# Issuing the K and V loads of a decode attention from GpSimd's software queue

## The chip, the cores and the metric

The kernel runs on one core of one Trainium2 chip. The metric is the device time of one execution in microseconds (us); before the change it is 1980.17 us, the median of three runs (1979.96 to 1980.22).

## The reference

Two blocks, A and B, of one-token attention over a long cache, each with 2 batches, 32 heads, 8192 cached positions and a head size of 192, in bf16:

```
q      = x @ wq                                  # x: 2 x 1 x 640, wq: 640 x 6144
scores = einsum("bhqd,bhkd->bhqk", q, k_cache) * 192 ** -0.5
p      = softmax(scores)
o      = einsum("bhqk,bhkd->bhqd", p, v_cache)
out    = o.transpose(0, 2, 1, 3).reshape(2, 1, 6144) @ wo     # wo: 6144 x 640
```

The two outputs are joined along the last axis. Nearly all the bytes are the four caches: K and V of one head of one batch are 8192 x 192 bf16 each, 3.146 MB, and there are 128 such pairs.

## The kernel before

One pair is a *unit*; units are counted u = 0 to 127 (NU = 128), two batches of a head after each other. K and V of a unit lie in SBUF as 128 partitions of 64 positions each, 24,576 bytes a partition. There are two K buffers (`kb`, NK = 2) and three V buffers (`vb`, NV = 3).

The work on a unit goes through all engines:

- **VectorE (DVE)** multiplies K by the broadcast query, in two halves (`dve_mul`, L230; signals "m0" and "m1"). It needs K(u), and frees K's buffer when "m1" is done. Later it gathers the sums (L233, "r0", "r1") and takes the maximum of each partition (L236, "d3").
- **TensorE (PE)** sums the products over the head size with an identity matrix (`pe_sum`, L295, "s0" and "s1"), and later multiplies the probabilities with V (`pe_pv`, L306, "pv"), which frees V's buffer.
- **GpSimd (POOL)** takes the maximum over all partitions (`pool_ar`, L220, called ar here) and later sums the exponentials over them (`pool_ls`, L224, called ls here).
- **ScalarE (ACT)** scales the maximum (L243), takes the exponential (L246, "exp") and evicts results.

Each engine works through its own list in order, and a wait holds everything behind it on that engine. DVE, ACT, PE and POOL have tables with a slot for each unit; `put(table, slot, order, ...)` files an operation, and the lists are written out by slot and, within a slot, by order. POOL's slot u holds ar(u) (order 0, waits for "d3" of u) and ls(u) (order 1, waits for "exp" of u). On PE the slot u holds the sums of u (order 0) and then the V product of u - 1 (order 2). The last two units differ: the sums of units 126 and 127 stand in slot 125 at order 1.8, and so ahead of the V product of unit 124, called pv(124) here.

SyncE (SP) issues all loads from one list, made at L425 to L454. K(u) waits for "m0" and "m1" of u - 2, V(u) for "pv" of u - 3. The order is K(0), wq(0), K(1), wo(0), V(0), K(2), V(1), K(3), V(2) and so on: the V of a unit stands behind the K of the next unit. K(127) is moved up behind K(126) and split into two halves; V(126) is split in two and V(127) in four pieces. Weights are set between: wq for 8 heads (1.97 MB, 3072 bytes a row, one buffer; waits for the last query projection from the one before, "pq") and wo for 4 heads (0.98 MB, 3840 bytes a row, two buffers; waits for "f5"). The query projections (`pe_q`, L287) run six units ahead of their use. The last two wo loads go into a K buffer at the end (L453).

K's loads count on one semaphore for each buffer (`ksem`), V's likewise (`vsem`).

The order of SP's list is made by these lines:

```python
for u in range(NU):
    order.append(("k", u))
    if u >= 1:
        order.append(("v", u - 1))
order.append(("v", NU - 1))
order.remove(("k", NU - 1))
order.insert(order.index(("k", NU - 2)) + 1, ("k", NU - 1))
```

Of the kernel before, what the change touches and what calls it, by code (L numbers as in the profile page):

```python
# [51 lines left out]
def build_kernel(nc, blocks, out):  # L52
# [5 lines left out]
    TH = T // 2  # L58
# [5 lines left out]
    NU = G * B  # L64
# [3 lines left out]
    NK = 2  # L68
    NV = 3
# [12 lines left out]
    def unit(u):  # L82
        g = u // B
        return g // Hn, g % Hn, u % B, g
# [7 lines left out]
    with ExitStack() as es:  # L92
        sb = lambda name, shape, dt: es.enter_context(nc.sbuf_tensor(name, shape, dt))
        ps = lambda name, shape, dt: es.enter_context(nc.psum_tensor(name, shape, dt))
        sem = lambda name: es.enter_context(nc.semaphore(name))

        kb = [sb(f"kb{i}", [128, T, Dh], BF16) for i in range(NK)]
# [28 lines left out]
        reg = {}  # L126
        S_sp = _Stream("sp", sem("s_sp"), reg)
# [4 lines left out]
        ksem = [sem(f"ksem{i}") for i in range(NK)]  # L132
        k2sem = {NU - 1: sem("k2sem1")}
# [10 lines left out]
        def key(name, *idx):  # L144
            for i in idx:
                if i < 0:
                    return None
            return (name,) + tuple(idx)

        vcount = [0] * NV  # L150
        for u in range(NU):
            reg[("k", u)] = (ksem[u % NK], 16 * (u // NK + 1))
            if u in VSPLIT:
                for i in range(len(VSPLIT[u]) - 1):
                    reg[("vp", u, i)] = (vpsem[u, i], 16)
            else:
                vcount[u % NV] += 1
                reg[("v", u)] = (vsem[u % NV], 16 * vcount[u % NV])
# [11 lines left out]
        def dma(out_ap, in_ap, s):  # L170
            return lambda eng: eng.dma_start(out_ap, in_ap).then_inc(s, 16)  # L171
# [4 lines left out]
        def sp_wq(w):  # L176
            blk = (w * HQ) // Hn
            h0 = (w * HQ) % Hn
            src = blocks[blk]["wq"].rearrange("(j c) n -> j c n", c=DC)[:, :, h0 * Dh:(h0 + HQ) * Dh]
            return dma(wqs[:], src, wqsem)  # L180
# [10 lines left out]
        def sp_wo(w):  # L191
            blk = (w * HO) // Hn
            h0 = (w * HO) % Hn
            src = blocks[blk]["wo"][h0 * Dh:(h0 + HO) * Dh, :].rearrange("(pr p i) n -> p pr (i n)", p=128, i=3)
            i = w - (NWO - NLATE)
            return dma(wo_tile(w).rearrange("p pr i n -> p pr (i n)"), src, wosem[w % 2] if i < 0 else wlsem[i])

        def sp_k(u, part=None):
            blk, h, b, g = unit(u)
            src = blocks[blk]["k"][b, h].rearrange("(p t) d -> p t d", p=128)  # L200
            if part is None:
                return dma(kb[u % NK][:], src, ksem[u % NK])
            if part == 0:
                return dma(kb[u % NK][:, 0:TH, :], src[:, 0:TH, :], ksem[u % NK])
            return dma(kb[u % NK][:, TH:T, :], src[:, TH:T, :], k2sem[u])

        def sp_v(u, t0=0, t1=T, sm=None):
            blk, h, b, g = unit(u)
            src = blocks[blk]["v"][b, h].rearrange("(p t) d -> p t d", p=128)
            return dma(vb[u % NV][:, t0:t1, :], src[:, t0:t1, :], vsem[u % NV] if sm is None else sm)  # L210

        def vcuts(u):
            c = VSPLIT[u]
            return list(zip(c[:-1], c[1:]))
# [23 lines left out]
        def dve_f2(g):  # L238
            s0 = 64 * (g % 2)
            return lambda eng: eng.reciprocal(rcT[(g // 2) % 2][s0:s0 + 64, :], lall[g % 2][s0:s0 + 64, :])  # L240
# [8 lines left out]
        def act_f1(g, b0, b1):  # L249
            hs = g % 2  # L250

            def fn(eng):
                eng.activation(o_sb[0:1, b0:b1, hs, :], ops[hs][0:1, b0:b1, 0:Dh], ACTF.Identity)  # L253
                return eng.activation(o_sb[32:33, b0:b1, hs, :], ops[hs][32:33, b0:b1, Dh:2 * Dh], ACTF.Identity)  # L254
            return fn
# [96 lines left out]
        pool_tab = [[] for _ in range(NSLOT)]  # L352

        def put(tab, slot, order, fn, waits, sig):
            tab[slot].append((order, len(tab[slot]), fn, waits, sig))

        for u in range(NU):
# [17 lines left out]
            else:  # L375
                cuts = vcuts(u)
                for i, (t0, t1) in enumerate(cuts):
                    put(pe_tab, u + 1, 2, pe_pv(u, t0 // 2, t1 // 2), (w0 if i == 0 else []) + [("vp", u, i)],
                        ("pv", u) if i == len(cuts) - 1 else None)

        for g in range(G):
            u1 = 2 * g + 1
            pp = g // 2
            w1 = [key("f3", pp - 1), ("init",)]
            if g == G - 1:
                put(act_tab, u1, 2, act_f1(g, 0, 1), [("pv", u1 - 1)] + w1, ("f1a", g))
                put(act_tab, u1 + 1, 2, act_f1(g, 1, 2), [("pv", u1), ("f1a", g)], ("f1", g))
            else:
                put(act_tab, u1 + 1, 2, act_f1(g, 0, 2), [("pv", u1)] + w1, ("f1", g))
            put(dve_tab, u1 + 1, 8, dve_f2(g), [("ls", u1), key("f4", pp - 2)], ("f2", g))  # L390
# [41 lines left out]
        order.insert(order.index(("k", NU - 2)) + 1, ("k", NU - 1))  # L432
        for kind, u in order:
            if kind == "k":
                S_sp.add(sp_k(u, 0 if u in k2sem else None), waits=[key("m0", u - NK), key("m1", u - NK)])
                if u in k2sem:
                    S_sp.add(sp_k(u, 1))
                if u == 0:
                    S_sp.add(sp_wq(0))
                w = u // UO  # L440
                if u % UO == 1 and w < NWO - NLATE:
                    S_sp.add(sp_wo(w), waits=[key("f5", ((w - 2) * HO + HO - 1) // 2 if w >= 2 else -1)])
                w = u // UQ
                if u % UQ == UQ - LEAD and w + 1 < NWQ:
                    S_sp.add(sp_wq(w + 1), waits=[key("pq", w * HQ + HQ - 1)])
            else:
                w = [key("pv", u - NV)]
                if u in VSPLIT:
                    for i, (t0, t1) in enumerate(vcuts(u)):
                        S_sp.add(sp_v(u, t0, t1, vpsem[u, i]), waits=w)  # L450
                else:
                    S_sp.add(sp_v(u), waits=w)
# [23 lines left out]
        for tab, S in ((dve_tab, S_dve), (act_tab, S_act), (pe_tab, S_pe), (pool_tab, S_pool)):  # L476
            evicted = None
            for slot in range(NSLOT):
                for _, _, fn, waits, sig in sorted(tab[slot], key=lambda e: (e[0], e[1])):
                    if sig is not None and sig[0] in ("pq", "f3", "f3a"):  # L480
                        waits = list(waits) + [evicted]
# [27 lines left out]
def bass_concat_heads__gqa_block_cached__mha_block_cached__decode_kernel(  # L509
    nc: bass.Bass,  # L510
    A_x: bass.AP,
    A_k_cache: bass.AP,
    A_v_cache: bass.AP,
    A_wq: bass.AP,
    A_wo: bass.AP,
    B_x: bass.AP,
    B_k_cache: bass.AP,
    B_v_cache: bass.AP,
    B_wq: bass.AP,
    B_wo: bass.AP,  # L520
    out: bass.AP,
):
    blocks = [
        dict(x=A_x, k=A_k_cache, v=A_v_cache, wq=A_wq, wo=A_wo),
        dict(x=B_x, k=B_k_cache, v=B_v_cache, wq=B_wq, wo=B_wo),
    ]
    build_kernel(nc, blocks, out)
# [28 lines left out]
```

## Time and profile before

| | |
|---|---|
| median of three runs | 1980.17 us |
| span of the profiled execution, first to last instruction | 1978.0 us |
| PE busy | 1651.6 us (84%) |
| DVE busy | 1056.0 us (53%) |
| ACT busy | 191.3 us (10%) |
| POOL busy | 121.6 us (6%) |
| read from HBM | 836.77 MB, 423 GB/s over the span |

The profiled execution's own time is not given apart from its span; the median of the runs is 2.2 us longer than the span.

The profile shows one execution. "Busy" counts the time that an engine works on instructions; issuing a DMA and waiting are not in it. The slices cut the span into 40 equal parts. The line of DMA gives the busy share of the 16 DMA engines in tenths, and the line below it what they moved. The DMA issues are listed with the median time from the issue to the landing, that is, until the semaphore tells that all has arrived; this holds the time in the queue too. In a timeline, a line has the start, the time, the engine, the line of the code, the operation, output and input with their shapes, and in brackets the idle time before it and what ended it. The chain of waits goes back from the last instruction: at each step to what released it.

### The profile page before, as it was taken

To read this page: it belongs to the slowest core of one execution; us is meant where nothing else is said; L and a number is where in the kernel's file an instruction comes from. 1 tells how busy PE (TensorE), PEld (TensorE's weight loads), DVE (VectorE), ACT (ScalarE), POOL (GpSimd) and SP (SyncE) were. 2 spreads that over 40 slices of the span, in tenths; PEclk is the share of its full clock that TensorE was granted. 3 is DMA by queue.
4 is the path that set the end of the run, shared out by engine and by line. 5 is a ranking of instruction groups with operands and counts; after the bars stand their busy time and mean duration, and the time that the engine had idled before them with its cause. 6 is when DMAs were issued, how large, how long until landed. Compare 5 with 4: busy or idle time off the path is not lost.

```text
span 1978.0 us, 18521 instructions
## 1 busy us (share of the span) xinstructions
PE 1651.6 (84%) x8076; PEld 816.4 (41%) x8076; DVE 1056.0 (53%) x706; ACT 191.3 (10%) x647; POOL 121.6 (6%) x269
## 2 busy tenths in 40 slices
PE   5988888879888888888888878888788977988878
PEld 2444444334444344443444434444344433444434
DVE  4554555545555455655555556555555555556552
ACT  0100101001010010010110101001001000010000
POOL 2200000000000000000000000000000000000001
PEclk9999999999999899998999999998999899998988
DMA  9999999999999999999999999999999999999995
GB/s 402 430 429 430 429 430 431 430 429 430 430 429 429 431 429 430 431 428 430 431 429 430 427 431 431 428 431 427 432 431 427 430 430 430 430 431 429 430 405 236
DMA packets 47856, 837.96 MB, mean 424 GB/s; under 512 B 5144, under 2 KB 5152, under 8 KB 14752
## 3 DMA queue, kind: packets, MB, share of 16 engines
q1 hardware_dynamic: 47188, 836.78, 99.0%
q8 instruction: 63, 1.03, 0.2%
q14 instruction: 17, 0.14, 0.0%
q10 hardware_dynamic: 588, 0.01, 0.0%
HBM read 836.77 MB, written 0.01 MB: 423 GB/s over the span
## 4 chain that ended last, share of the span: by engine, by line
DMA 74%; DVE 11%; issue 10%; PE 4%; POOL 0%; ACT 0%; SPq 0%; DVEq 0%
DMA kb<-in_B_k_cache_dram 38%; DMA kb<-in_A_k_cache_dram 35%; DVE prod L230 11%; PE scps L295 2%; PE ops L306 2%; DMA wqs<-in_A_wq_dram 1%; PE qps L287 0%; PE outps L341 0%; POOL mg L220 0%; PE qps L325 0%; DVE sc L233 0%; ACT qbc L266 0%; ACT pb L246 0%; ACT out_sb L270 0%; SPq L171 0%
## 5 line engine op out<-in xcount | busy, mean ns | idle before, releaser
L230 DVE TENSOR_TENSOR prod<-kb,qbc 128x6144 bf16<-128x6144 bf16 x256 | 848.2, 3355 | 530.4 <-DMA kb<-in_B_k_cache_dram 265.7
L295 PE MATMUL scps<-prod,ident 128*128 128x512 bf16 x3072 | 784.5, 414 | 289.7 <-DVE prod L230 289.4
L306 PE MATMUL ops<-vb,pb 128*33 128x384 bf16 x4096 | 716.4, 335 | 11.4 <-DMA vb<-in_A_v_cache_dram 6.8
L295 PEld LDWEIGHTS scps<-prod,ident 128*128 128x128 bf16 x3072 | 306.0, 105 | 753.7 <-DVE prod L230 370.9
L306 PEld LDWEIGHTS ops<-vb,pb 128*33 128x33 bf16 x4096 | 400.7, 100 | 315.4 <-issue 63.3
L233 DVE TENSOR_REDUCE sc<-scps 128x32 f32<-128x512 f32 x256 | 176.7, 690 | 345.0 <-PE scps L295 344.2
L220 POOL PARTITION_ALL_REDUCE mg<-mp x128 | 63.7, 498 | 1710.2 <-DVE mp L236 1282.2
L243 ACT ACTIVATE nb<-mg 128x1 f32<-128x1 f32 x128 | 26.0, 203 | 1369.1 <-POOL mg L220 1369.1
L287 PE MATMUL qps<-wqs,xbc 128*128 128x384 bf16 x320 | 65.5, 337 | 22.7 <-DMA wqs<-in_A_wq_dram 17.3
L314 PEld LDWEIGHTS qps<-ones,o_sb 33*128 33x128 f32 x372 | 67.1, 257 | 13.1 <-issue 13.1
L314 PE MATMUL qps<-ones,o_sb 33*128 33x1 f32 x372 | 69.7, 311 | 0.0
L224 POOL PARTITION_ALL_REDUCE lall<-rs x128 | 53.2, 416 | 116.9 <-ACT pb L246 116.9
L253 ACT ACTIVATE o_sb<-ops 1x384 f32<-1x384 f32 (+1 forms) x65 | 30.8, 475 | 248.6 <-PE ops L306 248.6
L246 ACT ACTIVATE pb<-sc,nb 128x64 bf16<-128x64 f32 x128 | 52.3, 408 | 14.0 <-PE ops L306 9.8
L287 PEld LDWEIGHTS qps<-wqs,xbc 128*128 128x128 bf16 x320 | 26.7, 99 | 56.5 <-issue 20.5
L266 ACT ACTIVATE qbc<-qps 128x384 bf16<-128x384 f32 x64 | 31.4, 490 | 141.7 <-PE qps L287 141.0
L254 ACT ACTIVATE o_sb<-ops 1x384 f32<-1x384 f32 (+1 forms) x65 | 31.0, 476 | 0.8
L236 DVE TENSOR_REDUCE mp<-sc 128x1 f32<-128x64 f32 x128 | 28.2, 220 | 4.4
L341 PE MATMUL outps<-wos,oTz 128*4 128x320 bf16 x168 | 27.4, 299 | 0.0
L246 ACT ACTIVATION_READ_ACCUMULATOR pb<-sc,nb 128x1 f32 x128 | 23.8, 186 | 0.0
L341 PEld LDWEIGHTS outps<-wos,oTz 128*4 128x4 bf16 x168 | 11.9, 84 | 17.6 <-issue 11.9
L240 DVE RECIPROCAL rcT<-lall 64x2 f32<-64x2 f32 x64 | 9.9, 154 | 12.7 <-POOL lall L224 11.7
(21 smaller groups left out, 33.2 us busy)
## 6 DMA issues: line engine op xcount, KB each, us to landing
kb<-in_A_k_cache_dram SPq DMA_DIRECT2D x64, 3072.0 KB, 22.5
vb<-in_A_v_cache_dram SPq DMA_DIRECT2D x64, 3072.0 KB, 29.5
kb<-in_B_k_cache_dram SPq DMA_DIRECT2D x63, 3072.0 KB, 22.5
vb<-in_B_v_cache_dram SPq DMA_DIRECT2D x62, 3072.0 KB, 29.8
wqs<-in_A_wq_dram SPq DMA_DIRECT2D x4, 1920.0 KB, 29.0
wos<-in_A_wo_dram SPq DMA_DIRECT2D x8, 960.0 KB, 24.4
wqs<-in_B_wq_dram SPq DMA_DIRECT2D x4, 1920.0 KB, 29.0
wos<-in_B_wo_dram SPq DMA_DIRECT2D x6, 960.0 KB, 24.4
```

What stands on the lines that cost most here:

```text
L220: return lambda eng: eng.partition_all_reduce(mg[u % 2][:], mp[u % 2][:], 128, bass.bass_isa.ReduceOp.max)
L224: return lambda eng: eng.partition_all_reduce(lall[g % 2][:, b:b + 1], rs[u % 2][:], 128, bass.bass_isa.ReduceOp.add)
L230: return lambda eng: eng.tensor_tensor(prod[hf][:], kb[u % NK][:, hf * TH:(hf + 1) * TH, :], q, ALU.mult)
L233: return lambda eng: eng.tensor_reduce(sc[u % 2][:, hf * TH:(hf + 1) * TH], scps[hf][:], AXL.X, ALU.add)
L246: return lambda eng: eng.activation(pb[u % 2][:, :, ::32], sc[u % 2][:].rearrange("p (j a) -> p j a", a=2), ACTF.Exp, bias=nb[u % 2][:], s ...
L254: return eng.activation(o_sb[32:33, b0:b1, hs, :], ops[hs][32:33, b0:b1, Dh:2 * Dh], ACTF.Identity)
L266: return lambda eng: eng.activation(qbc[qg % NQ][:], qps[:, 0:QW].rearrange("p (a d) -> p a d", a=2), ACTF.Identity)
L287: ins = eng.matmul(qps[:, 0:QW], xbc[blk][b][:, c, :], wqs[:, c, off:off + QW], start=(c == 0), stop=(c == DC - 1))
L295: ins = eng.matmul(scps[hf][:], ident[:], prod[hf][:, :, j * DG:(j + 1) * DG], start=(j == 0), stop=(j == NJ - 1))
L306: ins = eng.matmul(ops[(u // B) % 2][0:33, b, 0:QW], pb[u % 2][:, j, :], vv[:, j, :], start=(j == 0), stop=(j == TH - 1))
L314: ins = eng.matmul(oTps[:, 2 * i + b:2 * i + b + 1], o_sb[:, b, :, :].rearrange("p s (r i) -> p i (s r)", i=3)[:, i, :], ones33[:], start= ...
L341: ins = eng.matmul(outps[0:4, 0:NH2], oTz[:, pp % NZ, i, 2 - 2 * half:6 - 2 * half], wt[:, pr, i, half * NH2:(half + 1) * NH2], start=(fir ...
```

## The change

K(2) to K(125) and V(0) to V(125) are issued by GpSimd instead of SyncE, on its software queue. POOL's table gets them with the orders -4 to -2, and so ahead of ar in a slot: V(0) at the head of slot 0; in slot u, K(u+1) (waits for "m0" and "m1" of u - 1) and then V(u+1) (waits for "pv" of u - 2). In POOL's list K(u+2) and V(u+2) thus follow ls(u) and precede ar(u+1). SP's list keeps K(0), K(1), K(126), K(127), V(126), V(127) and all weights, with the waits they had. The four K loads that stay get a semaphore each, so that no semaphore is counted from two queues.

```diff
+        k1sem = {u: sem(f"k1sem{u}") for u in (0, 1, NU - 2, NU - 1)}
         for u in range(NU):
-            reg[("k", u)] = (ksem[u % NK], 16 * (u // NK + 1))
+            reg[("k", u)] = (k1sem[u], 16) if u in k1sem else (ksem[u % NK], 16 * (u // NK))
...
+        on_pool_k = range(2, NU - 2)
+        on_pool_v = range(0, NU - 2)
+        put(pool_tab, 0, -4, sp_v(0), [], None)
+        for u in range(NU):
+            if u + 1 in on_pool_k:
+                put(pool_tab, u, -3, sp_k(u + 1), [("m0", u - 1), ("m1", u - 1)], None)
+            if u in on_pool_v and u > 0:
+                put(pool_tab, u - 1, -2, sp_v(u), [key("pv", u - NV)], None)
...
             if kind == "k":
-                S_sp.add(sp_k(u, 0 if u in k2sem else None), waits=[key("m0", u - NK), key("m1", u - NK)])
+                if u not in on_pool_k:
+                    S_sp.add(sp_k(u, 0 if u in k2sem else None), waits=[key("m0", u - NK), key("m1", u - NK)])
...
             else:
                 w = [key("pv", u - NV)]
+                if u in on_pool_v:
+                    continue
```

More of the change, by code (lines that the diff above doesn't have):

```diff
@@ L200, in sp_k @@
             src = blocks[blk]["k"][b, h].rearrange("(p t) d -> p t d", p=128)
+            sm = k1sem.get(u, ksem[u % NK])
             if part is None:
-                return dma(kb[u % NK][:], src, ksem[u % NK])
+                return dma(kb[u % NK][:], src, sm)
             if part == 0:
-                return dma(kb[u % NK][:, 0:TH, :], src[:, 0:TH, :], ksem[u % NK])
+                return dma(kb[u % NK][:, 0:TH, :], src[:, 0:TH, :], sm)
             return dma(kb[u % NK][:, TH:T, :], src[:, TH:T, :], k2sem[u])
```

## Prediction

> **What bounds the kernel now.** I read the page first: the slices, the queues, the chain, the issues.
>
> ```profile
> DMA  9999999999999999999999999999999999999995
> GB/s 402 430 429 430 429 430 431 430 429 430 430 429 429 431 429 430 431 428 430 431 429 430 427 431 431 428 431 427 432 431 427 430 430 430 430 431 429 430 405 236
> ...
> q1 hardware_dynamic: 47188, 836.78, 99.0%
> ...
> DMA 74%; DVE 11%; issue 10%; PE 4%; POOL 0%; ACT 0%; SPq 0%; DVEq 0%
> ...
> kb<-in_A_k_cache_dram SPq DMA_DIRECT2D x64, 3072.0 KB, 22.5
> vb<-in_A_v_cache_dram SPq DMA_DIRECT2D x64, 3072.0 KB, 29.5
> ...
> xT<-in_A_x_dram ACTq DMA_DIRECT2D x2, 1.2 KB, 11.2
> ```
>
> The 16 DMA engines are full at 430 GB/s in every slice but the first and the last two, all through one hardware queue. A K load lands 22.5 us after its issue though it moves for only about 7.3: two other transfers stand before it. So the middle of the run is a full pipe, and only two things can move the time: the pace of a packet, and what happens where the pipe isn't full, at the two ends. The last units show both (timeline, some lines left out; units counted from 0, so these are units 124 to 127):
>
> ```profile
> 1896.75 6.63 DVE L230 TENSOR_TENSOR prod<-kb,qbc 128x6144 bf16<-128x6144 bf16 x2 [4.18 <-DMA kb<-in_B_k_cache_dram]
> ...
> 1903.40 15.43 SPq L171 DMA_DIRECT2D kb<-in_B_k_cache_dram  x3
> ...
> 1907.13 5.38 PE L306 MATMUL ops<-vb,pb 128*33 128x384 bf16 x32
> ...
> 1909.43 0.38 POOL L224 PARTITION_ALL_REDUCE lall<-rs  x1 [0.80 <-ACT pb L246]
> ...
> 1911.37 6.63 DVE L230 TENSOR_TENSOR prod<-kb,qbc 128x6144 bf16<-128x6144 bf16 x2 [2.99 <-DMA kb<-in_B_k_cache_dram]
> ...
> 1925.95 6.63 DVE L230 TENSOR_TENSOR prod<-kb,qbc 128x6144 bf16<-128x6144 bf16 x2 [3.13 <-DMA kb<-in_B_k_cache_dram]
> ...
> 1937.04 6.60 DVE L230 TENSOR_TENSOR prod<-kb,qbc 128x6144 bf16<-128x6144 bf16 x2
> 1937.14 6.71 POOL L220 PARTITION_ALL_REDUCE mg<-mp  x1 [12.71 <-DVE rcT L240]
> ```
>
> Multiplications start 14.62 us apart, each the moment its K lands: one K and one V, so 7.3 us a transfer (3.146 MB, 430.8 GB/s). The trace's packet records agree: a row of 24,576 bytes takes 913 ns, and each engine moves 8 rows of a transfer (7.30). From mul(127) at 1937.04 on, no K is awaited. The chain of waits, from there to the end:
>
> ```profile
> 1903.40 22.52 DMA kb<-in_B_k_cache_dram
> ...
> 1937.12 3.27 DVE prod L230
> 1940.38 0.05 issue
> 1940.43 7.99 PE scps L295 x24
> 1948.41 15.71 PE ops L306 x96
> ```
>
> The DMA stage thus ends with K(126), landing at 1925.9. All that follows is compute, 52.1 us of it; V(127) waits for pv(124), and the pipe is even empty from 1949 to 1954 (0 GB/s in that window).
>
> **Steady state: cost nothing, by these covers.** 124 K and 126 V loads leave SP; POOL issues K(u+2) behind ls(u) and V(u+2) behind that. The trace has ls(u) ending 12.0 to 14.3 us after mul(u) starts (13.1 in the unit above). The pipe then holds K(u+1) and V(u+1) and runs dry for K(u+2) at 3 x 7.3 = 21.9 in landing times, or 19.3 after K(u)'s landing as an issue time, taking off 2.6 us of latency (V(127)'s first half: issued about 1953.9 into an empty pipe, landed 1960.1, 3.65 of it data). 19.3 - 14.3 leaves at least 5.0 us, mostly 7.2. No row shows how long POOL spends on an issue; SP's takes 0.33 to 0.43. I take about 1 us, by that row: hidden. V(u+2) adds a wait on POOL for pv(u-1), which ends 14.8 to 19.9 after mul(u); the ar(u+1) behind it is due at about 25, so this wait is covered by 5 us, and V(u+2) itself isn't needed before 26.6.
>
> SP keeps 22 weight loads that no longer stand between K and V. They leave as soon as their own waits allow and share the pipe. How two queues share is shown by xT: 8 packets of 10 bytes per engine took 11.2 us beside K(0). One small packet passes for each 913 ns row, so the engines take turns by packet. The Trainium skill (DMA: Bandwidth & Descriptors, Queues, rings and completion order) says so too: each engine round-robins at packet granularity. wq has 40 packets of 121 ns per engine: 40 x 1.034 + 2.6 = 44 us beside POOL's rows. From pq(15) to pq(16), its window, there are 48 us (374.5 to 422.9; 47.6 at least in later groups). Hidden by 4; without that cover PE would stand for some us, eight times at most.
>
> **The start: nothing, barely.** V(0) and V(1) follow POOL's copies (end 17.15). K(2) was issued at 26.42 and now comes behind ls(0), which mul(1) holds until 38.42. Behind wq(0) (landed 17.3) stand K(1), V(0), V(1) at 7.3 each and wo(0), wo(1) at 2.3 each: 26.5 us, to 43.8. K(2)'s earliest landing stretch begins at 38.4 + 2.6 = 41.0. Cover 2.8 us, once.
>
> **The end: the loss.** Before, a V stood behind the next K (K(124), V(123), K(125), V(124), K(126)); POOL's order is K(u), V(u). So with a full pipe K(124) lands one transfer later, +7.3. Then, counted from its landing: V(124) lands at 7.3 and K(125) begins. SP's K(126) leaves after mul(124), 6.65, and joins at 9.25 on another queue. K(125) then has 5.35 left, takes turns with K(126), and lands at 9.25 + 10.7 = 19.95 (before: 14.6). K(126) shares its last 1.95 with V(125) and lands at 23.85; that is early, but DVE isn't free: mul(125) starts at 19.95, and mul to mul without a DMA wait is 11.45 (mul(125) start to the end of its maximum, 1922.81), so mul(126) starts at 31.4 and mul(127) 11.1 later (1925.95 to 1937.04) at 42.5. K(127) lands by 36.5, in time. Before, mul(127) stood 40.3 after K(124). Sum: 7.3 + 42.5 - 40.3 = **+9.5 us**. The compute behind it keeps its 41 us, for PE still works sum(126), sum(127), pv(124) in that order. If the hardware queue gave way entirely: K(126) at 29.2, mul(127) at 40.3, +7.3. If it had all: K(125) at 21.9, mul(127) at 44.45, +11.45.
>
> **The pace of POOL's packets** is the one unknown that counts 250 times; no row of before has the software queue. From 913 ns at 24,576 bytes and 121 ns at 3072, a packet costs 7.9 ns beside its bytes. Lower end: none of it is left, 250 x 8 x 7.9 ns = -15.8 us. Upper end: rows cut to the size of wo's packets, 3840 bytes at 149 ns: +4.4% on 250 x 7.3 = 1825 us, +81. I take the same pace, since the row and its spread over the engines don't change, and allow 0 to 100 ns a transfer for the software queue's own bookkeeping (0 to +25 us).
>
> **Rivals.**
> 1. *DVE holds POOL's issue.* The last timeline line is the evidence: ar, 0.35 us when DVE is idle, took 6.71 while mul(127) ran. If descriptor writing is held in the same way, a K issue that isn't done when mul(u+1) starts (14.6) waits until 21.3, 2.0 past the 19.3, plus about 1 to issue. ls ends at 13 or later in about a third of the units: 42 x 3 = +126, less where a late K moves the next multiplication: +100, 2090 us. Against it: ar reads SBUF, descriptor writing need not. The Trainium skill (SBUF — State Buffer, SBUF: two separate sides) warns of it: a DMA issued from GpSimd stalls while DVE runs an operation in a two-port mode, since its descriptors can't be written. Its section Who interferes with whom excepts tensor_tensor, whose second input blocks GpSimd's reads only, which it calls inferred; with that exception the rival gives nothing. The 6.71 us row agrees for the read; no run here shows the write.
> 2. *Rows are cut*: +81 + 9.5, 2071 us. Against it: the hardware queue's DMA instruction keeps 24,576 bytes as one element.
> 3. *Faster: the packet's fixed 7.9 ns goes* because descriptors lie ready in a ring. It decides from 9.5 us / 2000 packets = 4.8 ns a packet; in full -15.8 + 9.5 = -6.3, 1974 us. Against it: 14.61 us for 16 rows already leaves no gap, and the same engines do the work.
> 4. *No change*: the tail is lost in part only (the pipe a little faster, as in 3, or K(126) served last): 1982 us.
>
> **How the numbers follow.** The profiled span is 1978.0 us; the median is 1980.17, so 2.2 us lie around it, and I add the sum to the median: 1980.17 + 9.5 = **1989.7 us**. Chances: the forecast at equal pace (1987.5 to 1992) 0.52; the same with the software queue's bookkeeping (to 2015) 0.18; rival 1 0.07, rival 2 0.06 (both above the range); rival 3 0.08; rival 4 0.09. The range takes the first two, rival 4 in part: 1981 to 2016. What a measurement can tell is 0.2%, 4 us: faster 0.08, same 0.09, slower 0.83.
>
> **What would show it.** Right: 24,576-byte packets at 913 ns in a software queue; multiplications still 14.6 apart; mul(125) to mul(126) over 11 us with no wait for K at the second; mul(127) to the end again 41 us. Wrong: gaps in DMA share near mul(u+1) (rival 1); short packets (2); a spacing under 14.55 (3). The forecast fails if POOL takes over 6 us for an issue, or if weights come late for pq.

## The result and the profile after

The changed kernel takes **1989.99 us** (median of 4 runs, 1989.54 to 1990.22) beside 1980.2 of the kernel before on the same chip: ratio 1.0049, 95% interval 1.0035 to 1.0064, 9.8 us slower. The forecast was 1989.7. The profiled execution took 1990.22 us with a span of 1988.5.

The page of the changed kernel, the lines that answer to those of before:

```profile
GB/s 400 433 428 429 430 429 430 429 429 431 430 430 430 429 430 427 430 429 430 429 427 430 430 430 426 430 429 429 430 426 429 428 429 430 427 431 425 429 406 173
...
q0 software_dynamic: 36000, 786.45, 92.3%
q1 hardware_dynamic: 11188, 50.34, 6.3%
...
DMA 56%; PE 18%; DVE 14%; issue 7%; ACT 2%; POOL 2%; SPq 0%; DVEq 0%
...
L172 POOL DMA_DIRECT2D kb<-in_A_k_cache_dram x62 | 35.4, 571 | 0.0
...
kb<-in_A_k_cache_dram POOLq DMA_DIRECT2D x62, 3072.0 KB, 17.3
...
wqs<-in_A_wq_dram SPq DMA_DIRECT2D x4, 1920.0 KB, 42.9
```

The bytes have moved to the software queue, and the pipe is as full as before; only the last slice has fallen, from 236 to 173 GB/s. A K load lands 17.3 us after its issue instead of 22.5: it is issued later, not served faster. The weights on SP's queue need 42.9 us instead of 29.0. In the packet records of the trace, all 32,000 rows on the software queue have the size and the median of before: 24,576 bytes, 913 ns.

The timeline of the changed kernel, units 124 to 127 (start, time, engine, line, operation):

```profile
1904.46 6.63 DVE L232 TENSOR_TENSOR prod<-kb,qbc 128x6144 bf16<-128x6144 bf16 x2 [4.60 <-DMA kb<-in_B_k_cache_dram]
1904.49 0.53 POOL L172 DMA_DIRECT2D vb<-in_B_v_cache_dram  x1 [2.56 <-PE ops L308]
...
1911.12 21.66 SPq L172 DMA_DIRECT2D kb<-in_B_k_cache_dram  x3
...
1923.64 6.63 DVE L232 TENSOR_TENSOR prod<-kb,qbc 128x6144 bf16<-128x6144 bf16 x2 [7.54 <-DMA kb<-in_B_k_cache_dram]
1927.05 8.03 PE L297 MATMUL scps<-prod,ident 128*128 128x512 bf16 x24 [6.82 <-DVE prod L232]
...
1935.99 6.62 DVE L232 TENSOR_TENSOR prod<-kb,qbc 128x6144 bf16<-128x6144 bf16 x2
...
1947.36 6.60 DVE L232 TENSOR_TENSOR prod<-kb,qbc 128x6144 bf16<-128x6144 bf16 x2
```

Mul(124) starts 7.7 us later than before (1896.75). Mul(125) follows 19.2 us after it instead of 14.6, and its idle time before (7.54) ended with the landing of K(125). Mul(126) has no wait for K in its brackets: K(126) had landed, and DVE was the late one. From mul(127) to the end of the span there are 41 us, as before.

The same stretches in every run, from the starts of the multiplications in each trace (us; a transfer is 7.3). The number of the run is that of the next section; the last two columns go to the last instruction:

| kernel (run) | mul(8) | mul(8) to (120) | mul(124) | 124 to 125 | 125 to 126 | 126 to 127 | 127 to end | 124 to end |
|---|---|---|---|---|---|---|---|---|
| before | 129.2 | 1708.3 | 1896.75 | 14.6 | 14.6 | 11.1 | 41.0 | 81.3 |
| after | 138.8 | 1706.8 | 1904.46 | 19.2 | 12.4 | 11.4 | 41.1 | 84.0 |
| SP, new order (1) | 136.6 | 1708.6 | 1904.04 | 14.6 | 14.6 | 12.4 | 40.0 | 81.6 |
| POOL, old order (2) | 137.1 | 1706.8 | 1902.35 | 19.2 | 11.4 | 12.6 | 40.0 | 83.1 |
| all on POOL, old order (3) | 137.8 | 1707.2 | 1903.33 | 14.6 | 14.6 | 11.6 | 41.2 | 82.0 |
| all on POOL, new order (4) | 138.9 | 1707.0 | 1904.36 | 14.6 | 14.6 | 12.2 | 39.8 | 81.3 |
| run 3 with V(1) first (5) | 140.2 | 1706.7 | 1905.31 | 14.6 | 15.4 | 11.2 | 41.0 | 82.3 |
| run 2 with V(1) first (6) | 140.2 | 1706.9 | 1905.56 | 19.2 | 11.4 | 12.6 | 40.0 | 83.2 |
| run 3, K(2) to K(4) on SP (7) | 134.6 | 1706.7 | 1899.79 | 14.6 | 14.6 | 11.9 | 39.7 | 80.8 |
| run 2, K(2) to K(4) on SP (8) | 135.5 | 1706.5 | 1900.41 | 19.2 | 11.6 | 12.7 | 40.0 | 83.5 |
| SP, V(124) later (9) | 129.4 | 1708.6 | 1896.56 | 14.6 | 10.4 | 12.5 | 40.0 | 77.4 |
| SP, V(123) later too (10) | 129.4 | 1708.6 | 1896.45 | 11.7 | 12.5 | 10.7 | 43.7 | 78.5 |

In 112 steady units no kernel differs from before by more than 1.8 us, and those with the software queue are the shorter ones. They load wo(1), 2.3 us of the pipe, ahead of unit 8 instead of behind it; with that allowed for, they are 0.5 to 1.1 us longer, about 5 ns for each of 224 transfers at most. Nearly all the loss lies at the two ends. The new order's share of it is there from the start (mul(8) 7.4 us late in run 1): each K is one V later all through, and nothing at the end wins that back.

### The profile page after: what moved, and what is told of

It is laid out like the page before. It is cut to its first block, busy times and chain, and to the rows that moved or that the text cites. A ratio compares the mean times of both kernels' runs of the same rounds, so it can differ in the third digit from the quotient of the medians.

```text
span 1988.5 us, 18521 instructions
## 1 busy us (share of the span) xinstructions
PE 1654.3 (83%) x8076; PEld 816.3 (41%) x8076; DVE 1056.0 (53%) x706; ACT 191.4 (10%) x647; POOL 236.5 (12%) x519
## 4 chain that ended last, share of the span: by engine, by line
DMA 56%; PE 18%; DVE 14%; issue 7%; ACT 2%; POOL 2%; SPq 0%; DVEq 0%
DMA kb<-in_B_k_cache_dram 28%; DMA kb<-in_A_k_cache_dram 27%; PE scps L297 16%; DVE prod L232 11%; DVE sc L235 2%; PE ops L308 2%; ACT pb L248 1%; POOL mg L222 1%; DMA wqs<-in_A_wq_dram 1%; POOL lall L226 1%; DVE mp L238 1%; ACT nb L245 1%; PE outps L343 0%; PE qps L289 0%; PE qps L327 0%
## 5 line engine op out<-in xcount | busy, mean ns | idle before, releaser
L297 PE MATMUL scps<-prod,ident 128*128 128x512 bf16 x3072 | 792.6, 417 | 309.1 <-DVE prod L232 308.7
L222 POOL PARTITION_ALL_REDUCE mg<-mp x128 | 56.7, 443 | 1171.6 <-DVE mp L238 956.3
L289 PE MATMUL qps<-wqs,xbc 128*128 128x384 bf16 x320 | 65.4, 337 | 22.6 <-DMA wqs<-in_A_wq_dram 17.2
L172 POOL DMA_DIRECT2D vb<-in_A_v_cache_dram x64 | 34.1, 533 | 217.4 <-PE ops L308 212.2
L172 POOL DMA_DIRECT2D vb<-in_B_v_cache_dram x62 | 32.7, 528 | 216.7 <-PE ops L308 209.3
L268 ACT ACTIVATE qbc<-qps 128x384 bf16<-128x384 f32 x64 | 31.4, 490 | 142.1 <-PE qps L289 141.4
L172 POOL DMA_DIRECT2D kb<-in_A_k_cache_dram x62 | 35.4, 571 | 0.0
L172 POOL DMA_DIRECT2D kb<-in_B_k_cache_dram x62 | 35.2, 568 | 0.0
## 6 DMA issues: line engine op xcount, KB each, us to landing
kb<-in_A_k_cache_dram POOLq DMA_DIRECT2D x62, 3072.0 KB, 17.3
kb<-in_B_k_cache_dram POOLq DMA_DIRECT2D x62, 3072.0 KB, 17.3
wqs<-in_A_wq_dram SPq DMA_DIRECT2D x4, 1920.0 KB, 42.9
```

Of the source, the lines that this page charges most:

```text
L222: return lambda eng: eng.partition_all_reduce(mg[u % 2][:], mp[u % 2][:], 128, bass.bass_isa.ReduceOp.max)
L289: ins = eng.matmul(qps[:, 0:QW], xbc[blk][b][:, c, :], wqs[:, c, off:off + QW], start=(c == 0), stop=(c == DC - 1))
L297: ins = eng.matmul(scps[hf][:], ident[:], prod[hf][:, :, j * DG:(j + 1) * DG], start=(j == 0), stop=(j == NJ - 1))
```

## The experiments

The theory was the prediction's: (a) V(u) ahead of K(u+1) puts K(126) one transfer later, and (b) two queues taking turns delay K(125). Rival A: the software queue itself costs the time. Rival B: order is the whole loss.

**1. The order alone, on SyncE.** The kernel before, with its list in POOL's order:

```diff
-        order = []
-        for u in range(NU):
+        order = [("k", 0), ("k", 1), ("v", 0), ("v", 1)]
+        for u in range(2, NU):
             order.append(("k", u))
-            if u >= 1:
-                order.append(("v", u - 1))
-        order.append(("v", NU - 1))
+            order.append(("v", u))
```

Expected: 

> All loads on SyncE's hardware queue as before, but in POOL's order (K(u), V(u) instead of V(u-1) behind K(u)). Theory (the order puts K(126) one transfer, 7.3 us, later; two queues at the end cost 2.2 us more): +7.3 us, 1987.5, with multiplication 126 waiting for K and 127 standing 40.3 us after 124, as before. Rival A (the software queue itself is the cost, by its start or its pace): no change, 1980.2. Rival B (order is the whole loss): +9.8, 1990.

Measured: 1987.25 us beside 1979.87, ratio 1.0037 (1.0022 to 1.0051), +7.4. Its timeline, multiplications 124 and 126:

```profile
1904.04 6.63 DVE L230 TENSOR_TENSOR prod<-kb,qbc 128x6144 bf16<-128x6144 bf16 x2 [4.56 <-DMA kb<-in_B_k_cache_dram]
...
1933.25 6.63 DVE L230 TENSOR_TENSOR prod<-kb,qbc 128x6144 bf16<-128x6144 bf16 x2 [4.17 <-DMA kb<-in_B_k_cache_dram]
```

Mul(124) is 7.3 us late without any software queue, and mul(126) still follows 29.2 us behind it, on K's landing. Rival A can't explain this part; rival B would have wanted 2.4 more. (Mul(126) to mul(127) took 1.3 more than before and the rest 1.0 less; the part on why the prediction was right says why.)

**2. The old order, on GpSimd.** The changed kernel with each V one slot later:

```diff
-                put(pool_tab, u - 1, -2, sp_v(u), [key("pv", u - NV)], None)
+                put(pool_tab, u, -2, sp_v(u), [key("pv", u - NV)], None)
```

Expected: 

> The changed kernel with the V loads one slot later on GpSimd, so that V(u-1) stands behind K(u) as on SyncE before; K(126), K(127), V(126) and V(127) still on SyncE. Theory: only the sharing at the end is left, K(125) lands about 19.5 us after K(124) instead of 14.6, and mul(126) starts about 31.5 after mul(124) instead of 29.2: +2.2 us, 1982.4 (multiplication 124 at about 1897 as before). Rival A: the loss stays, about 1990. Rival B: 1980.2.

Measured: 1987.77 us beside 1979.87, ratio 1.0041 (1.0026 to 1.0056), +7.9: a miss. The end was as expected (19.2 us from mul(124) to mul(125)), but mul(124) was 5.6 late. The windows of its start (busy time of PE, PEld, DVE, ACT, POOL; PE clock, DMA share, GB/s) show where, and the lines of POOL below them what held K(2):

```profile
30.00:34.00 4.00, 1.17 (x7) 0.47 (x5) 3.57 (x3) 0.00 (x0) 2.52 (x1) 1.00 0.90 373
34.00:39.00 5.00, 3.01 (x9) 1.34 (x10) 3.88 (x2) 1.51 (x5) 4.18 (x4) 0.50 0.18 71
39.00:44.00 5.00, 5.00 (x21) 2.04 (x19) 0.69 (x1) 0.00 (x0) 0.28 (x1) 0.82 0.98 359
...
35.66 2.47 POOL L226 PARTITION_ALL_REDUCE lall<-rs  x1 [0.81 <-ACT pb L248]
38.00 0.74 POOL L172 DMA_DIRECT2D kb<-in_A_k_cache_dram  x1
```

From 34 to 39 us the pipe moves 71 GB/s. K(2) stands behind ls(0) on POOL, which mul(1) held, and was issued at 38.00. In the changed kernel V(1) filled this time; in the old order only V(0) is in front. The prediction put the cover at 2.8 us; one transfer of 7.3 less makes -4.5, and by the packet records the DMA engines stand idle for 4.7 us of 30 to 44. The other 0.9 of the 5.6 is not explained.

**3 and 4. All on GpSimd, in both orders.** K(126), K(127) and V(126) go to POOL as well, so that no K load shares at the end. The main lines:

```diff
-        on_pool_k = range(2, NU - 2)
-        on_pool_v = range(0, NU - 2)
+        on_pool_k = range(2, NU)
+        on_pool_v = range(0, NU - 1)
...
```

Expected of the old order: 

> Old order and, beyond it, K(126), K(127) and V(126) on GpSimd too, so that the last K loads share with nobody; SyncE keeps K(0), K(1), V(127) and the weights. Theory: neither term is left: +0.0 to +0.6 us (K(127) is issued behind ls(125) and its second half may be 0.2 late; 0.4 may come from the start), 1980.2 to 1980.8; K(124), K(125) and K(126) land 14.6 apart. Rival A (the software queue costs something for each of 250 loads): slower by that, over 1982. Rival B: 1980.2.

Expected of the new order: 

> As the run with all on GpSimd, but in the changed kernel's order, K(u), V(u). Theory: the order's term alone, +7.3 to +7.9 us, 1987.5 to 1988.1; K(124) to K(126) 14.6 apart, mul(127) 40.3 after mul(124). Rival A: as the changed kernel, 1990, since nothing of the software queue is undone. Rival B (order is the whole loss): 1990.

Measured: old order 1986.37 us beside 1979.87, ratio 1.0031 (1.0018 to 1.0045), +6.5, a miss, in the main for the cause just told: its window from 34 to 39 us has 68 GB/s. Of the 6.6 us that mul(124) is late, 4.9 are idle time of the pipe there; 1.7 stay open. New order 1987.18, ratio 1.0038 (1.0025 to 1.0051), +7.3 as expected. The multiplications 124 and 125 of the run in the new order:

```profile
1904.36 6.63 DVE L232 TENSOR_TENSOR prod<-kb,qbc 128x6144 bf16<-128x6144 bf16 x2 [3.18 <-DMA kb<-in_B_k_cache_dram]
1918.96 6.63 DVE L232 TENSOR_TENSOR prod<-kb,qbc 128x6144 bf16<-128x6144 bf16 x2 [2.97 <-DMA kb<-in_B_k_cache_dram]
```

With one queue at the end, the 19.2 us are 14.6 again: the sharing, not the software queue, had stretched them. And all on the software queue costs no more than all on the hardware queue in the same order (1987.18 and 1987.25). That leaves rival A nothing that these runs can tell.

**5 and 6. V(1) put first again.** Against the gap at the start, in runs 3 and 2:

```diff
         put(pool_tab, 0, -4, sp_v(0), [], None)
+        put(pool_tab, 0, -4, sp_v(1), [], None)
...
-            if u in on_pool_v and u > 0:
+            if u in on_pool_v and u > 1:
```

Expected of all on GpSimd: 

> All on GpSimd in the old order, and V(1) put back at the head beside V(0). Theory now: the run without it lost about 5 us where the pipe stood empty from 34.5 to 39.5 us, since only V(0) stood behind ls(0); with V(1) there the pipe stays full, and mul(124) to mul(127) keeps its 40.8: 1980.6 to 1981.6. Rival (in the old order, the software queue loses in the steady part, where K(124) was 6.6 late with 4.8 explained): 1982 to 1983. If the gap isn't the cause: 1986, as without.

Expected with the last K loads on SyncE: 

> The changed kernel in the old order (K(126) and after on SyncE), and V(1) put back at the head beside V(0). Theory: the start's gap goes, the sharing at the end stays (mul(124) to mul(127) about 43.0 instead of 40.3): +2.8 and 0.4 to 1.0 from the steady part, 1983 to 1983.8. Rival (sharing costs nothing): as the run with all on GpSimd. If the gap isn't the cause: 1987.5.

Measured: 1988.98 us beside 1979.73, ratio 1.0046 (1.0031 to 1.0061), and 1990.72, ratio 1.0055 (1.004 to 1.007). Both are slower still, against every expectation. The windows of the first of them:

```profile
58.00:65.00 7.00, 7.00 (x39) 3.57 (x38) 4.16 (x6) 0.00 (x0) 2.33 (x1) 1.00 0.93 400
65.00:71.00 6.00, 6.00 (x33) 3.00 (x32) 4.72 (x3) 1.52 (x6) 5.20 (x3) 1.00 0.01 4
```

The gap at 34 us is gone, and one of 6 us stands at 65 (8 GB/s there in the second run). With V(1) taken out from between them, K(2) and K(3) land 8 us apart, so mul(3) starts as soon as DVE is free and holds ar(2) for 6.70 us; ls(2) and with it K(4) leave at 70.44. The pipe hadn't one transfer too few at one place; POOL issues too late for the old order as long as multiplications run back to back.

**7 and 8. The early K loads on SyncE.** In runs 3 and 2, K(2) to K(4) stay on SP, where they wait for the multiplication alone (the line of run 3; run 2 has `range(5, NU - 2)`):

```diff
-        on_pool_k = range(2, NU)
+        on_pool_k = range(5, NU)
...
```

Expected of all else on GpSimd: 

> All on GpSimd in the old order but K(0) to K(4), which SyncE issues as it did before, 12 us ahead of ls; no V is moved. Theory (POOL's K loads leave only behind ls, which a multiplication holds at the start, so the old order needs one transfer more in the pipe than it has; putting V(1) first only moved the gap to 65 to 71 us): no gap at either place, mul(124) 0.5 to 1.7 later than before, mul(124) to mul(127) about 40.8: 1980.5 to 1982. Rival (the old order loses on the software queue wherever its K loads are issued): a gap behind K(5), 1985 to 1987.

Expected with the last K loads on SyncE: 

> The changed kernel in the old order, with K(0) to K(4) on SyncE: the sharing of the last K loads (K(126) on SyncE beside K(125) on GpSimd) alone. Theory: as the run beside it, plus mul(124) to mul(127) of about 43 instead of 40.8: 1982.3 to 1984. Rival (sharing costs nothing): the same time as the run beside it.

Measured: 1982.4 us beside 1979.76, ratio 1.0014 (1.0005 to 1.0024), and 1985.16, ratio 1.0025 (1.0015 to 1.0035). Multiplications 124 to 126 of the second:

```profile
1900.41 6.63 DVE L237 TENSOR_TENSOR prod<-kb,qbc 128x6144 bf16<-128x6144 bf16 x2 [3.15 <-DMA kb<-in_B_k_cache_dram]
1919.59 6.63 DVE L237 TENSOR_TENSOR prod<-kb,qbc 128x6144 bf16<-128x6144 bf16 x2 [8.56 <-DMA kb<-in_B_k_cache_dram]
1931.20 6.62 DVE L237 TENSOR_TENSOR prod<-kb,qbc 128x6144 bf16<-128x6144 bf16 x2
```

With 123 and 121 K loads and nearly all V loads still on the software queue, the loss falls from 6.5 to 2.6 us and from 7.9 to 5.4. Between the two runs lie 2.8 us, put down to sharing: 19.2 us from mul(124) to mul(125) again, then mul(126) without a wait for K. The two intervals overlap, so it is the profiles (mul(124) to mul(127) 43.5 and 41.1) that carry this. The size is less sure than the fact: the medians of runs 2 and 3 differ by 1.4, of 6 and 5 by 1.7, of the changed kernel and run 4, each against its own before, by 2.5. Runs 7 and 8 are 0.4 and 1.2 us above their ranges: mul(124) is 3.0 late in the first, of which dips of the pipe near 39 and 55 us explain about 0.7. The rest stays open.

**9 and 10. The other way: K earlier at the end.** On SyncE alone, V(124) behind K(126); in the second run V(123) behind K(125) too, with its product behind the sums of 125:

```diff
+        order.remove(("v", NU - 4))
+        order.insert(order.index(("k", NU - 2)) + 1, ("v", NU - 4))
```

Expected of the first: 

> The kernel before, on SyncE alone, with V(124) moved behind K(126). By the same account of the end, K(126) lands one transfer earlier (21.9 us after K(124)), but DVE is free only 11.45 after mul(125), at 26.1; mul(127) stands 37.1 after mul(124) instead of 40.3: -3.2 us, 1976.8. If the order of the last loads weren't what sets the end, no change: 1980.

Expected of the second: 

> As the run with V(124) behind K(126), and V(123) moved behind K(125) as well, with pv(123) behind the sums of unit 125 on PE and one small transpose (f3 of the last pair but one) behind the sums of 127. K(125) lands 7.3 after K(124), mul(125) starts at 11.45, mul(126) at 22.9, mul(127) at 34.0 to 36 after mul(124): -4 to -6.3 us, 1973.6 to 1976. If PE waits for V(123) ahead of the sums of 126, nothing beyond the -3.2: 1976.8.

Measured: 1975.84 us beside 1979.73, ratio 0.9981 (0.9972 to 0.9991), -3.9, and 1975.39, ratio 0.9979 (0.997 to 0.9988), -4.3. The first run's multiplications 125 to 127:

```profile
1911.14 6.63 DVE L230 TENSOR_TENSOR prod<-kb,qbc 128x6144 bf16<-128x6144 bf16 x2 [3.05 <-DMA kb<-in_B_k_cache_dram]
...
1921.49 6.62 DVE L230 TENSOR_TENSOR prod<-kb,qbc 128x6144 bf16<-128x6144 bf16 x2
...
1933.99 6.60 DVE L230 TENSOR_TENSOR prod<-kb,qbc 128x6144 bf16<-128x6144 bf16 x2
```

One V moved makes the kernel 0.2% faster than before: mul(126) no longer waits for K. This is the order's term with the opposite sign, as far as DVE lets it: mul(127) comes 3.05 us earlier, and the rest is the stretch behind it. The second V brings mul(127) 2.7 us earlier (1931.28), but behind it the end is 43.7 us away instead of 40.0: the transpose f3, moved there with it (2.25), and V products that take 17.45 us instead of 15.78, with a granted clock of 0.70 from 1945 to 1950 where the first run has 1.00. The gain is given back on PE.

## Why the prediction was right

- **What bounds the kernel.** Right: the steady stretch is the same within 0.1%, and what moved are the ends.
- **POOL's issues hidden.** Right: 0.53 to 0.57 us each (estimated 1).
- **The weights.** 42.9 us to land (estimated 44), and PE's wait for wq is 17.2 us, once, at the start, as before (17.3).
- **The start.** Right: the share of the pipe is 0.96 from 30 to 40 us. That the cover was thin is what runs 2 and 3 showed; taking one transfer from it opened a gap of 4.7 and 4.9 us where its 2.8 gave 4.5.
- **The end, term by term.** K(124) one transfer late: 7.3 predicted, 7.7 measured (0.4 open). Mul(125) after mul(124): 19.95 and 19.2. Mul(126): 31.4 and 31.5. Mul(127): 42.5 and 42.9. K(126) landed at 25.1 instead of 23.85, which cost nothing, since DVE was later still. V(125) landed at 29.2, four transfers, as a full pipe would have it. Two small errors cancel: K(125) came 0.8 early, and mul(125) to mul(126) took 12.35 instead of 11.45, since the sums on PE took 8.03 us where they took 7.04 in unit 125 of before; PE's granted clock was 0.53 from 1925 to 1933.
- **Luck in the last microsecond.** The sums of one unit take 6.0 us where the clock granted over them is 1.00, and up to 8.3 where it is 0.64, and which of the last units gets which differs between runs. The prediction took the lengths of before. Its 41 us behind mul(127) held because the sums of 127 were slow in both (7.99 and 8.13 us); in runs 1, 2 and 4 they took 6.9 to 7.0, the sums of 126 took 7.8 to 8.2 instead, and 40 us were left. So single terms of the end are good to about 1 us, and a sum within 0.3 of the measured one is closer than they allow.
- **The sum.** 9.5 predicted; the medians differ by 9.8 and the spans by 10.5.
- **The order without the sharing**, +7.3 in the prediction's text for the case that the hardware queue gives way: runs 1 and 4 measured 7.4 and 7.3.
- **Packets' pace**, bounded from -15.8 to +81 us: it was the same, 913 ns. Rivals 2 and 3 fall with it, and rival 4 with the measured end. The allowance of 0 to 100 ns a transfer for bookkeeping came from no row; the steady units leave room for about 5.
- **Rival 1** (DVE holds POOL's issue) falls too: 96 of the 250 issues, all of them of V, lie wholly within one half of a multiplication and took 0.527 to 0.537 us, as the one at 1904.49 above. The Trainium skill (SBUF — State Buffer, Who interferes with whom) excepts tensor_tensor and marks it as inferred; this trace agrees with the exception, by these times and by the steady units, which are at most 1.1 us longer where the rival asked for about 100. But the hold itself is real where POOL reads (ar, 6.70 us in run 5), and it came back by another way, which the prediction saw only as ls(0): an issue *behind* a held instruction is late though it isn't held itself.

What failed are expectations behind the prediction, for the old order on POOL. Those of runs 2 and 3 undid the loss at the end and forgot that the start's cover, worked out before, consisted of V(1); those of runs 5 and 6 put V(1) back and missed that the gap moves on. Two parts stay open: 0.9 to 3.0 us by which mul(124) is late in the old order on POOL beyond the gaps seen, and the exact price of sharing.

## What to carry to other kernels

When a full pipe is handed to another queue, its steady pace says little; ask which transfer the last stage waits for, how many others now stand before it, and whether a second queue takes turns with it there. Loads issued from an engine with work of its own leave when that work lets them, so an order of loads that was just deep enough on SyncE can run the pipe dry at the start. At the end of a pipe that is bound by DMA, what isn't needed until after the last compute stage belongs behind what starts it: here, moving one V load gained 3.9 us, while no run that changed the queue gained anything.

## What of the hardware was not expected

A load on the software queue costs what it costs on the hardware queue: 913 ns a row of 24,576 bytes, 7.3 us a transfer, and 0.53 to 0.57 us of GpSimd for 3.1 MB. That two queues take turns by packet and not by bytes was expected, but not how far it goes: wo(0) and wo(1), 0.98 MB each in packets of 3840 bytes, stood behind K(1), which landed at 28.1 us, and landed at 44.1 and 60.1 beside the V and K rows. That is 16 us each where one takes 2.3 alone: an engine has 16 packets of 149 ns of it, and if each lets a row of 913 ns pass, that is 17.0 us.
